# Score rounds earlier, value units together and the gelu table sooner, in one stage of an attention and MLP kernel

## The chip, the cores and the metric

One Trainium2 chip, one core of it. The metric is the device time of one execution in microseconds (us); lower is better. Engines: PE (TensorE, matmuls), PEld (its weight loads, which overlap), DVE (VectorE), ACT (ScalarE), POOL (GpSimd) and SP (SyncE, here only DMA issues).

## The reference, cut to what matters

```python
def _attn_ref(q_l, k_l, v_l, q_g, k_g, v_g):      # B=8, H=8, Sl=512, Sg=32, D=64
    k_all = concat([k_g, k_l]); v_all = concat([v_g, v_l])      # 544 positions
    out_g = softmax(scale * q_g @ k_all.T) @ v_all              # global queries see all
    s_ll  = scale * q_l @ k_l.T, where |pos_i - pos_j| <= 32, else -1e9
    s_lg  = scale * q_l @ k_g.T
    out_l = softmax(concat([s_lg, s_ll])) @ concat([v_g, v_l])  # local queries: window and globals
    return concat([out_g, out_l])

x = out.transpose(0, 2, 1, 3).reshape(B * 544, 512)
h = x @ w_in                         # w_in 512 x 2048
g = h * (1 / (1 + exp(-1.702 * h)))  # quick gelu
return g @ w_out                     # w_out 2048 x 512
```

## The kernel before

Each of the eight batches is worked on in two quads of four heads (`u` 0 and 1). For a batch, attention yields `xL`, the 512 local rows turned (four chunks of 128 columns: quad 0 gives chunks 0 and 1, quad 1 chunks 2 and 3). The first product (`h_mm`, L613) multiplies it with `w_in`, 16 steps `fc` of four matmuls of 128x512; ACT applies gelu from PSUM into `gT` (L618). The second product (`o_mm`, L653) multiplies `gT` with `w_out`: four output tiles `tci` of 128 rows, each a sum over 16 matmuls, issued in four steps of four matmuls. In `osteps(0, (tci, f4), ...)` the pair names tile and step; step `(tci, 3)` is the last of its tile and is followed by `o_out`, which copies the PSUM bank to `ob` (on ACT through `on_act`, L113, or on DVE through `nc.vector.tensor_copy`, L770) and has SP issue four stores.

The order on every engine is the order in which the program's lines issue instructions; it is written by hand (`tc.manual_schedule()`), and semaphores are put in where data or buffers depend. So a wait of an instruction holds everything behind it on its engine.

The change lies in the stage where the second product of batch 0 is mixed with the attention of batch 1. Its two quads are `a` and `c` (class `Wide`). The methods of a quad, with the lines that the profile shows:

- `Tk`, `Tq`, `ext` (L510, L502, L315, L505, L536 to L543, on DVE; parts on ACT, L113): bring keys and queries of the quad into place.
- `S(rnd)` (L558): one of two rounds of scores, 24 small matmuls that use 32 rows of the array each, into four PSUM banks in two tiles of two banks (a `spair()`; there is one, so each round reuses the banks of the round before).
- `X(rnd)` (L569): two exponentials on ACT, one for each two-bank tile, into `E[rnd]`.
- `M(rnd)` (L574, DVE): multiplies `E[rnd]` with the window's mask.
- `U(unit)` (L584): a value unit, 24 matmuls that use 32 columns each; unit 0 sums the rows of `E`, units 1 and 2 multiply with the values.
- `R` (L460, L462, L464, DVE): turns the sums of unit 0 (`sT`), takes reciprocals, and turns them back (`rs`).
- `XL(h)` (L469, DVE): unit 1 + h times `rs`, into `xL`.
- `Gm` (L595) and `G` (L474 to L477, DVE): the global queries, 20 matmuls, and their normalising.

PSUM has eight banks: the `spair()`'s four, and four in a pool (`pbank`) that second product tiles (`op`), `a`'s units (`ov`) and first product steps (`hp`) take in turn. `c`'s units and both `Gm` are written into a `spair()` of their own: bank 0 has `c.U(0)`, bank 1 both `Gm`, banks 2 and 3 `c.U(1)` and `c.U(2)`.

`exp_table()` and `gelu_table()` do one tiny activation on ACT, so that the table which the next activations need is loaded (ACT_TABLE_LOAD) at that place. `behind(x)` (L626) has POOL copy two elements of `x`; POOL issues the loads written behind it, those of batches 2 and 3, only then.

After this stage comes the first product of batch 1: eight matmuls on chunks 0 and 1 of `xL` (`kcs` (0, 1)), four on chunk 2, four on chunk 3, for the steps `fc` 0 to 3; then steps 4 to 15.

Of the kernel before, what the change touches and what calls it, by code (L numbers as in the profile page):

```python
# [20 lines left out]
def kernel(  # L21
# [12 lines left out]
    nc = tc.nc  # L34
# [40 lines left out]
    def load(b, us=(0, 1), kq=True):  # L75
        if b not in loaded:
            loaded[b] = (ld.tile([128, 2, 16 * D], BF16, name="rk"),
                         ld.tile([128, 2, 16 * D], BF16, name="rq"))
        if kq:
            s = slice(us[0], us[-1] + 1)  # L80
            nc.gpsimd.dma_start(out=loaded[b][1][:, s], in_=qf[b][:, s])
            nc.gpsimd.dma_start(out=loaded[b][0][:, s], in_=kf[b][:, s])
# [8 lines left out]
    def load_v(b, hs=slice(0, 8)):  # L91
        if b == 2:
            nc.gpsimd.memset(v_view(b, 5)[:, :, :, :, D:], 1.0)
        vt = v_view(b, 5).rearrange("p u j c d -> p (u j) c d")
        vs, vg = (x[b].rearrange("h s d -> s h d") for x in (v_l, v_g))
        for c in range(5):
            n = 128 if c == 2 else 96
            nc.gpsimd.dma_start(out=vt[0:n, hs, c, :D], in_=vs[FIRST[c] : FIRST[c] + n, hs])  # L98
            if c != 2 and b != 1:
                nc.gpsimd.dma_start(out=vt[96:128, :, c, :D], in_=vg)  # L100
# [176 lines left out]
    xL = {}  # L277

    def pbank(name):
        return psP.tile([128, 512], F32, name=name, tag="p")  # L280


    def spair():
        return [psS.tile([128, 2, 512], F32, name="s4", tag="s%d" % i) for i in range(2)]

    def bank(pair, j):
        return pair[j // 2][:, j % 2, :]
# [316 lines left out]
    gTs, ops = {}, {}  # L604
# [12 lines left out]
    def gelu(out_, in_):  # L617
        nc.scalar.activation(out_, in_, AF.Gelu_apprx_sigmoid)  # L618
# [6 lines left out]
    def behind(x):  # L625
        nc.gpsimd.tensor_copy(spot_p, x)  # L626

    def gelu_table():
        gelu(spot[:, 0:1], spot[:, 1:2])
# [16 lines left out]
    def o_mm(i, st, out=True):  # L646
        tci, f4 = divmod(st, 4)
        first = (i, tci) not in ops
        if first:
            ops[i, tci] = pbank("op")  # L650
        op = ops[i, tci]
        for fc in range(4 * f4, 4 * f4 + 4):
            nc.tensor.matmul(op, lhsT=gTs[i][:, fc, tci * 128 : tci * 128 + 128],  # L653
                             rhs=w_out_sb[:, fc, :], start=(first and fc == 4 * f4), stop=(fc == FC - 1))
        if f4 == 3 and out:
            o_out(i, tci, op)
# [102 lines left out]
    def tile_out(i, tci, ob):  # L759
        rows = out[i * S + Sg : (i + 1) * S].rearrange("(r t) m -> t r m", t=16)  # L760
        for j in range(4):
            nc.sync.dma_start(out=rows[4 * tci + j], in_=ob[32 * j : 32 * j + 32])
# [3 lines left out]
    def o_out(i, tci, op, copy=on_act):  # L766
        if tci % 2 == 0:
            obs[i, tci // 2] = moe.tile([128, 4, HM], F32, name="ob", bufs=3)
        ob = obs[i, tci // 2][:, tci % 2 * 2 : tci % 2 * 2 + 2].rearrange("p h m -> p (h m)")
        copy(ob, op)  # L770
        tile_out(i, tci, ob)

    a, c = Quad(0), Quad(1)
# [44 lines left out]
    pt = spair()  # L818
# [13 lines left out]
    pt = spair()  # L832
# [22 lines left out]
    def osteps(i, *sts):  # L855
        for tci, f4 in sts:
            o_mm(i, 4 * tci + f4)

    nq = {1: (Wide(2), Wide(3)), 2: (Wide(4), Wide(5))}
    a, c = nq[1]  # L860
# [3 lines left out]
    transpose_g(2, 4)  # L864
    a.ext((0, 1), on_act)
    a.ext((2, 3))
    osteps(0, (0, 1), (0, 0), (1, 1), (1, 0), (2, 1), (2, 0))
    a.S(0)
    a.X(0)
    copy_vg1()  # L870
# [1 line left out]
    c.Tq()  # L872
    c.ext()
    a.M(0)
    osteps(0, (0, 2), (1, 2), (2, 2))
    a.S(1)
    a.X(1)
    a.M(1)
    osteps(0, (3, 1), (3, 0))
    c.S(0)  # L880
    c.X(0)
    osteps(0, (0, 3), (1, 3))
    c.M(0)
    o_mm(0, 11, False)
    o_out(0, 2, ops[0, 2], nc.vector.tensor_copy)
    c.S(1)
    c.X(1)
    for unit in range(3):
        a.U(unit)
    a.R()  # L890
    c.M(1)
    behind(c.E[1][0:1, 0, 32:34])
    load(2, (0,))
    load_g(4, 8)
    load(2, (1,))
    load(3)
    load_v(2)
    osteps(0, (3, 2), (3, 3))
    pt = spair()
    a.XL(0)  # L900
    a.XL(1)
    a.Gm(bank(pt, 1)[:, 0:128])
    c.Gm(bank(pt, 1)[:, 128:256])
    c.U(0, bank(pt, 0))
    c.R()
    c.U(1, bank(pt, 2))
    c.U(2, bank(pt, 3))
    c.XL(0)
    c.XL(1)
    gTs[1] = moe.tile([128, FC, TB], BF16, name="gT")  # L910
    hps = [pbank("hp") for _ in range(4)]
    for kcs in ((0, 1), (2,), (3,)):
# [7 lines left out]
    pt = spair()  # L920
# [3 lines left out]
    a, c = nq[2]  # L924
# [154 lines left out]
    for i in range(1, B):  # L1079
        if i > 1:  # L1080
            for fc in range(FC):
# [3 lines left out]
                if i + 1 < B:  # L1085
                    c = nq[i + 1][1]
# [107 lines left out]
```

## Time and profile before

| | us |
|---|---|
| median of 3 runs | 288.90 (288.88 to 288.94) |
| the profiled execution: its own time | 288.66 |
| the profiled execution: its span | 286.6 |
| PE busy | 277.6 (97% of the span) |
| DVE busy | 204.6 (71%) |
| ACT busy | 184.4 (64%) |
| POOL busy | 94.1 (33%) |
| the stage from 31.8 to 48.3: PE busy | 16.27 of 16.50 |
| 48.3 to 55.8: PE busy | 6.85 of 7.50 |
| 55.8 to 66.6: PE busy | 10.75 of 10.80 |

The granted TensorE clock stands at 9 (90% or more) in every slice of the page but the last. Times in rows of the timeline are counted from the start of the span: start, duration, engine, line, operation, output tile <- input tiles, shapes, how many were merged into the row, and in brackets how long the engine had been idle before and who ended that. A chain row has start, duration and what ran. Matmuls are pipelined: a matmul of 512 columns shows 0.38 us but the next starts 0.22 after it.

### The profile page before, as it was taken

The page shows a single profiled execution, that of the slowest core. Times are in us where ns is not written, and L with a number is a line of the kernel's source. Part 1 is how long each engine was busy: PE and PEld are TensorE (multiplying, and loading weights), DVE is VectorE, ACT ScalarE, POOL GpSimd, SP SyncE. Part 2 cuts the span into 40 slices and gives each one's busy share as a digit, 9 for nine tenths or more (in the row PEclk, how much of TensorE's full clock was granted, in tenths as well). Part 3 has the DMA queues.
Part 4 walks back from the last instruction along what each step waited for, and adds up shares of the span by engine and source line. Part 5 has one row for each costly group of instructions (what it writes and reads, how often), then busy time and mean ns, then how long its engine had stood idle before and what let it go on. Part 6 is the DMA issues. An engine that isn't in the chain of part 4 may idle for free.

```text
span 286.6 us, 8822 instructions
## 1 busy us (share of the span) xinstructions
PE 277.6 (97%) x3704; PEld 178.6 (62%) x3727; DVE 204.6 (71%) x494; ACT 184.4 (64%) x296; POOL 94.1 (33%) x140
## 2 busy tenths in 40 slices
PE   7899999999999999999999999999999999999994
PEld 6544445544554488646884588647874588458883
DVE  7671457788689898679957997779957697363452
ACT  4847657388778784778559774877658761873440
POOL 8974550766936002920086004800040000000000
PEclk9999999999999999999999999999999999999999
DMA  7999994999999802993059703940122003200213
GB/s 204 167 200 211 202 143 66 153 224 144 161 170 174 150 3 57 91 185 59 12 84 160 139 2 78 107 58 5 29 54 70 2 3 76 73 0 2 73 44 106
DMA packets 59543, 28.23 MB, mean 98 GB/s; under 512 B 47472, under 2 KB 50032, under 8 KB 59504
## 3 DMA queue, kind: packets, MB, share of 16 engines
q0 software_dynamic: 51664, 17.57, 55.1%
q1 hardware_dynamic: 7264, 9.31, 11.8%
q10 hardware_dynamic: 576, 0.79, 0.8%
q8 instruction: 29, 0.48, 0.7%
q14 instruction: 10, 0.08, 0.1%
HBM read 36.31 MB, written 8.91 MB: 158 GB/s over the span
## 4 chain that ended last, share of the span: by engine, by line
PE 91%; DVE 2%; DMA 2%; POOL 1%; issue 1%; ACT 1%; DVEq 0%; POOLq 0%
PE hp L613 38%; PE px L724 13%; PE py L724 9%; PE op L653 9%; PE x L724 6%; PE s L558 6%; PE ov L584 5%; PE s L613 2%; DMA rk<-in_k_l_dram 2%; DVE xL L469 1%; ACT e L382 1%; PE og L595 1%; DVE rs L464 1%; DVE sT L460 0%; PE s L354 0%
## 5 line engine op out<-in xcount | busy, mean ns | idle before, releaser
L613 PE MATMUL hp<-xL,w_in_sb 128*128 128x512 bf16 x465 | 104.6, 379 | 1.2 <-DVE xL L469 0.4
L613 PEld LDWEIGHTS <-w_in_sb 128*128 128x128 bf16 x576 | 56.1, 98 | 60.3 <-issue 0.7
L618 ACT ACTIVATE gT<-hp 128x512 bf16<-128x512 f32 x120 | 69.9, 598 | 20.8 <-PE hp L613 19.3
L569 ACT ACTIVATE e<-s 128x1016 bf16<-128x1016 f32 (+1 forms) x56 | 53.3, 1003 | 22.1 <-PE s L558 22.0
L724 PEld LDWEIGHTS <-gs 128*128 128x128 bf16 x480 | 46.2, 98 | 6.4
L697 DVE TENSOR_TENSOR gs<-gT 128x512 bf16<-128x512 bf16 (+1 forms) x90 | 30.4, 365 | 17.6 <-ACT gT L618 17.3
L574 POOL TENSOR_TENSOR e<-e,mask 128x1760 bf16<-128x1760 bf16 x4 | 13.3, 3320 | 82.6 <-ACT e L569 82.6
L98 POOL DMA_DIRECT2D v<-in_v_l_dram x40 | 31.2, 781 | 15.4 <-PE og L595 4.3
L724 PE MATMUL py<-wsum,gs 128*128 128x256 bf16 x240 | 30.3, 273 | 0.0
L574 DVE TENSOR_TENSOR e<-e,mask 128x1712 bf16<-128x1712 bf16 (+1 forms) x24 | 25.2, 1049 | 6.0 <-ACT e L569 5.9
L653 PE MATMUL op<-w_out_sb,gT 128*128 128x512 bf16 x122 | 28.8, 380 | 0.5 <-issue 0.3
L510 DVE STREAM_TRANSPOSE kT<-rk 128x512 f32<-128x512 f32 x14 | 14.6, 1044 | 15.3 <-DMA rk<-in_k_l_dram 15.3
L653 PEld LDWEIGHTS <-gT 128*128 128x128 bf16 x128 | 11.8, 98 | 13.9
L724 PEld LDWEIGHTS <-gT 128*128 128x128 bf16 x192 | 18.0, 98 | 2.7
L724 PE MATMUL px<-w_out_sb,gT 128*128 128x256 bf16 x160 | 19.2, 273 | 0.0
L724 PE MATMUL px<-w_out_sb,gs 128*128 128x256 bf16 x160 | 19.1, 273 | 0.0
L469 DVE TENSOR_TENSOR xL<-ov,rs 128x512 bf16<-128x512 f32 x27 | 17.9, 687 | 0.8 <-PE ov L436 0.4
L694 DVE TENSOR_TENSOR gs<-gT 128x1024 bf16<-128x1024 bf16 (+1 forms) x30 | 17.4, 580 | 0.0
L558 PEld LDWEIGHTS <-kT 32*128 32x128 bf16 x672 | 12.6, 93 | 7.3 <-issue 5.9
L113 ACT ACTIVATE ob<-px 128x512 f32<-128x512 f32 x10 | 6.0, 599 | 15.2 <-DVE zz L746 15.2
L558 PE MATMUL s<-q,kT 32*128 32x160 bf16 (+1 forms) x448 | 14.9, 246 | 0.0
L100 POOL DMA_DIRECT2D v<-in_v_g_dram x24 | 13.9, 580 | 1.8 <-DMA rq<-in_q_l_dram 1.7
(149 smaller groups left out, 343.4 us busy)
## 6 DMA issues: line engine op xcount, KB each, us to landing
out_dram<-ob SPq DMA_DIRECT2D x128, 64.0 KB, 2.3
rq<-in_q_l_dram POOLq DMA_DIRECT2D x5, 512.0 KB, 8.4
rk<-in_k_l_dram POOLq DMA_DIRECT2D x5, 512.0 KB, 10.6
v<-in_v_l_dram POOLq DMA_DIRECT2D x24, 96.0 KB, 4.7
w_in_sb<-in_moe_w_in_dram POOLq DMA_DIRECT2D x8, 256.0 KB, 8.2
w_out_sb<-in_moe_w_out_dram POOLq DMA_DIRECT2D x4, 512.0 KB, 10.4
rq<-in_q_l_dram POOLq DMA_DIRECT2D x5, 256.0 KB, 7.9
rk<-in_k_l_dram POOLq DMA_DIRECT2D x5, 256.0 KB, 7.9
```

Source lines behind the costliest of these rows:

```text
L98: nc.gpsimd.dma_start(out=vt[0:n, hs, c, :D], in_=vs[FIRST[c] : FIRST[c] + n, hs])
L469: nc.vector.tensor_mul(self.x[:, 2 * self.u + h, :], self.st[1 + h], self.st["rs"])
L510: nc.vector.transpose(flat[:, 0:Sl].rearrange("p (r t) -> p t r", t=16), loaded[self.b][0][:, self.u].bitcast(F32))
L558: nc.tensor.matmul(bank(self.ps, j)[:, at : at + n], lhsT=self.k[p, KEYS[c] : KEYS[c] + 128, e], rhs=qs[p, :, :, e], start=(e == 0), stop= ...
L569: nc.scalar.activation(self.E[rnd][:, 2 * i : 2 * i + 2, :n], self.ps[i][:, :, :n], AF.Exp, scale=scale)
L574: eng.tensor_mul(e, e, mask[:, rnd : rnd + 1, :n].to_broadcast([128, 4, n]))
L613: nc.tensor.matmul(hp[:, : width(i)], lhsT=w_in_c[:, fc // 4, kc, fc % 4 // 2, :, fc % 2], rhs=(xL[i] if i < B else xG)[:, kc, :], start=( ...
L618: nc.scalar.activation(out_, in_, AF.Gelu_apprx_sigmoid)
L653: nc.tensor.matmul(op, lhsT=gTs[i][:, fc, tci * 128 : tci * 128 + 128], rhs=w_out_sb[:, fc, :], start=(first and fc == 4 * f4), stop=(fc = ...
L694: nc.vector.tensor_tensor(sums[i][2][:, g, :n], t[:, g, 0, :n], t[:, g, 1, :n], ALU.add)
L697: nc.vector.tensor_tensor(sums[i][k][:, g, : n // 2], x[:, g], y[:, g], op)
L724: nc.tensor.matmul(out_, lhsT=lv[:, g, tt * 128 : tt * 128 + 128], rhs=rv[:, g, :], start=(g == 0 and k in ((1, 3, 4, 6) if self.apart els ...
```

## The change

It reorders the stage. The rounds `a.S(0)`, `a.S(1)`, `c.S(0)` and `c.S(1)` come one to three steps of the second product earlier, so that two steps lie between one round and the next. The output tile 0 is evicted by DVE and tile 2 by ACT, which were the other way round. `a.U(0)` and `a.R()` stay behind the last round, but `a.U(1)`, `a.U(2)` come two steps after (2,3), in one group with `c`'s units and both `Gm`; `Gm` stands behind `c`'s units, which it preceded. Steps (3,2) and (3,3) come behind all of them, just ahead of the first product. `gelu_table()` is called ahead of (3,1), where before the table was loaded with the first gelu. `behind` waits for `a`'s second part of `xL` in place of `c`'s masked exponentials.

```diff
-    osteps(0, (0, 1), (0, 0), (1, 1), (1, 0), (2, 1), (2, 0))
+    osteps(0, (0, 1), (0, 0), (1, 1), (1, 0), (2, 1))
     a.S(0)
     a.X(0)
     copy_vg1()
...
     a.M(0)
-    osteps(0, (0, 2), (1, 2), (2, 2))
+    osteps(0, (2, 0), (0, 2))
     a.S(1)
     a.X(1)
     a.M(1)
-    osteps(0, (3, 1), (3, 0))
+    osteps(0, (1, 2), (2, 2))
     c.S(0)
     c.X(0)
-    osteps(0, (0, 3), (1, 3))
+    o_mm(0, 3, False)
+    o_out(0, 0, ops[0, 0], nc.vector.tensor_copy)
+    osteps(0, (1, 3))
     c.M(0)
-    o_mm(0, 11, False)
-    o_out(0, 2, ops[0, 2], nc.vector.tensor_copy)
     c.S(1)
     c.X(1)
-    for unit in range(3):
-        a.U(unit)
+    a.U(0)
     a.R()
+    osteps(0, (2, 3))
+    gelu_table()
+    osteps(0, (3, 1), (3, 0))
     c.M(1)
-    behind(c.E[1][0:1, 0, 32:34])
+    a.U(1)
+    a.U(2)
+    a.XL(0)
+    a.XL(1)
+    behind(xL[1][0:1, 1, 0:2])
     load(2, (0,))
     load_g(4, 8)
     load(2, (1,))
     load(3)
     load_v(2)
-    osteps(0, (3, 2), (3, 3))
     pt = spair()
-    a.XL(0)
-    a.XL(1)
-    a.Gm(bank(pt, 1)[:, 0:128])
-    c.Gm(bank(pt, 1)[:, 128:256])
     c.U(0, bank(pt, 0))
     c.R()
     c.U(1, bank(pt, 2))
     c.U(2, bank(pt, 3))
+    a.Gm(bank(pt, 1)[:, 0:128])
+    c.Gm(bank(pt, 1)[:, 128:256])
     c.XL(0)
     c.XL(1)
+    osteps(0, (3, 2), (3, 3))
```

## The prediction

> **What bounds the kernel now.** I read the page first (engines, the chain that ended last), then the chain between 28 and 66 us, then the timeline of that stretch engine by engine.
>
> ```profile
> PE 277.6 (97%) x3704; PEld 178.6 (62%) x3727; DVE 204.6 (71%) x494; ACT 184.4 (64%) x296; POOL 94.1 (33%) x140
> ```
>
> TensorE is the bound nearly everywhere, so the change is worth what it does to TensorE's waits, no more. The chain of batch 0's second product:
>
> ```profile
> 40.68 0.56 PE s L558 x24
> 41.25 0.16 issue
> 41.41 1.67 PE op L653 x7
> 43.08 0.18 PE s L558 x2
> 43.26 0.02 issue
> 43.28 0.64 PE s L558 x19
> 43.92 2.70 PE op L653 x12
> 46.61 0.56 PE s L558 x23
> ```
>
> Two waits stand here. The first is inside c.S(0): two score matmuls at 43.01 to 43.08, the others only from 43.28. (The "issue" 0.16 before 41.41 is no wait: eight weight loads and seven matmuls are recorded there, so one record is missing.) The second is at the next first product:
>
> ```profile
> 41.34 1.89 ACT L569 ACTIVATE e<-s 128x992 bf16<-128x992 f32 x2 [1.33 <-PE s L558]
> 43.98 1.93 ACT L569 ACTIVATE e<-s 128x1016 bf16<-128x1016 f32 x2 [0.75 <-PE s L558]
> 50.31 1.28 DVE L469 TENSOR_TENSOR xL<-ov,rs 128x512 bf16<-128x512 f32 x2
> 51.50 0.71 DVE L460 STREAM_TRANSPOSE sT<-s 128x512 f32<-128x512 f32 x1
> 53.35 1.29 DVE L469 TENSOR_TENSOR xL<-s,rs 128x512 bf16<-128x512 f32 x2
> 54.09 1.89 PE L613 MATMUL hp<-xL,w_in_sb 128*128 128x512 bf16 x8 [0.44 <-DVE xL L469]
> 55.41 1.28 ACT L618 ACT_TABLE_LOAD   x1 [4.57 <-PE hp L613]
> ```
>
> The first exp row ends at 43.23 and the stalled scores go on at 43.28: a score round writes the same two bank pairs as the round before and waits until its exponentials have read them. The product starts at 51.75; its eight matmuls on the first two chunks need 8 x 0.216 = 1.73 us, to 53.48, and the ninth starts at 54.09, 0.05 after c's first xL. So 0.60 us of wait (the row says 0.44, as it counts from the modelled end). 0.216 is (59.27 - 55.82) / 16 from the starts of two rows of the same product. Between 54.09 and 66.6 I find no gap in TensorE.
>
> **Part 1, score rounds sooner.** Before, an S round is followed by 12, 8 and 12 matmuls of the second product; after, by 8, 8 and 8 (rows (2,0),(0,2); (1,2),(2,2); (0,3),(1,3)). TensorE's own period with 12 is 40.62 - 37.34 = 3.28 us, so with 8 it is 3.28 - 4 x 0.216 = 2.41. ScalarE's loop is longer: two exponentials 1.89 or 1.93, 0.05 to release the banks, and 0.70 from the release to the next exponential (43.28 to 43.98): 2.64 or 2.68.
> - a.S(0) starts 4 matmuls sooner, 37.34 - 0.86 = 36.48 (its operands are ready: the last DVE copy ends at 35.85, ACT's at 35.90). Its exponentials run 37.22 to 39.15, banks free at 39.20; TensorE is at the second pair at 38.90. Wait 0.30.
> - c.S(0): 2.64 - 2.41 = 0.23. Its DVE operands, tied to a DMA and not moved, end at 41.14 and it starts at 41.6.
> - c.S(1): 2.68 - 2.41 = 0.27.
> Sum 0.80 against 0.27 before: **+0.53**. The trace bounds this well, as the same wait stands in it once (0.26); I allow 0.15 either way.
>
> **Part 2, evictions.** Output tile 0 goes to VectorE's copy (0.68), tile 2 to ScalarE (0.60). VectorE's copy starts at some 43.5, ahead of c.M(0), which waits for the exponentials until 44.5: hidden. ScalarE's eviction of tile 1 falls at 44.4 to 45.0, before c.S(1)'s exponentials can start at 45.2: hidden; without that cover 0.60 would lengthen ScalarE's loop. Tile 2's follows the last exponential, 47.0 to 47.6. Bank reuse, as the built program lists it, adds no wait: a.U(1) takes tile 1's bank, a.U(2) that of a.U(0), and the product's last bank is tile 3's, asked for 1.30 us (six matmuls) into the product and free some 0.85 after tile 3's last matmul (49.83 + 0.22 to 50.85 + 0.05 before).
>
> **Part 3, value units together.** c.S(1) now ends so that a.U(0) starts at 45.06. Then 4 + 8 matmuls of the second product to 48.14, and in one block a.U(1), a.U(2), c.U(0..2) at 0.37 each (50.55 to 50.91 for one), then the two Gm. The number of changes between tiled and full matmuls stays at five blocks. VectorE gets a.U(1) at 48.8 (last matmul 48.56, 0.22 long, 0.06 to VectorE), multiplies xL twice (0.60 each in a row), and starts c's transpose sT at 50.03, done at 50.74.
>
> In the built program's list of waits the first weight load of a.Gm now waits for that transpose: a.Gm writes the second bank of the pair whose first bank holds c.U(0). Before, Gm stood ahead of c.U(0) and had no such wait. TensorE arrives at 48.24 + 5 x 0.37 = 50.07 and goes on at 50.79: **+0.72**. Queued behind it on TensorE: both Gm, (3,2), (3,3) and the product, everything. No row of before shows this wait. Its lower bound is 0 (the transpose already done), its upper 1.0 (two xL at the 0.69 of a single one and a later a.U(1)); I take the computed value, as all its parts are rows of the same instructions, 0.2 either way.
>
> [...]
>
> **Part 4, cover for c's xL.** (3,2), (3,3) now stand between c's value units and the product. c's first xL ends at about 52.6, and the third chunk is wanted at 52.98 + 1.73 = 54.7: the wait of 0.60 goes, **-0.60**. The second Gm waited 0.09 (50.35 to 50.44) for c.M(1), now done at 48.4: -0.07 over its usual 0.02.
>
> **Part 5, gelu table and loads.** The load (1.28) and one 0.20 activation run at 47.6 to 49.1, where ScalarE waits for tile 3 until 53.2. ScalarE's first gelu comes some 0.7 us sooner (56.71 to about 56.0), but TensorE had no wait for gelu there: 0 on the path. Uncovered it would cost 1.28. `behind` now waits for a's second xL, 50.1, against 50.39 for c's mask: POOL's loads start 0.3 sooner. SP's stores of tiles 0 to 2 move forward, into 44 to 49.5; tile 3's 256 KB goes from 51 to about 54, into the loads. Priced in the first rival.
>
> **Sum.** +0.53 + 0.72 - 0.60 - 0.07 = +0.58, which I take as +0.6. The profiled execution took 288.66 us (span 286.6 and 2.06 around it): 289.26 by it. The median of the runs shown is 288.90, 0.24 more, and the forecast goes by it: **289.5**.
>
> **Rivals.**
> - *Late loads* (slower still). Batch 2's keys arrive at 58.23 and hold VectorE, then ScalarE:
>
> ```profile
> 58.23 1.05 DVE L510 STREAM_TRANSPOSE kT<-rk 128x512 f32<-128x512 f32 x1 [2.16 <-DMA rk<-in_k_l_dram]
> 60.68 0.31 ACT L113 ACTIVATE q<-qgT 128x128 bf16<-128x128 bf16 x1 [0.99 <-DVE qgT L243]
> 62.01 0.59 ACT L618 ACTIVATE gT<-hp 128x512 bf16<-128x512 f32 x1
> ```
>
>  The last row frees the bank that the thirteenth step of the product takes at 62.72: 0.07 to spare. TensorE comes 0.6 later, so the keys must be over 0.67 us late to cost anything. The store of tile 3 at the queue's share (9.31 MB took 11.8% of 286.6 us) is 0.9 us of all DMA engines, less the 0.3 sooner and less what it frees at 51. Against: probably 0.1 to 0.3 late. Price 0.3, time 289.8.
> - *No wait at a.Gm* (not slower). If a.Gm finds the transpose done, or bank by bank counts, only scores cost: 288.9 + 0.53 - 0.67 = 288.76. It decides from a transpose that ends before 50.07, that is, from a.U(1) 0.7 us earlier against c.U(2). Against: VectorE's rows add up without slack, and the wait is listed.
> - *ScalarE keeps pace*: if the loop took 2.41 like TensorE's, scores cost -0.27: 288.9 - 0.27 + 0.72 - 0.67 = 288.68. For: the exponentials start before a round's last score. Against: 43.23 to 43.28 to 43.98 in the trace.
> - Both of the last two: 288.9 - 0.94 = 287.96, the only way to faster.
> That the change doesn't do what it says is open for "sooner" alone: c.S(1) comes 12 matmuls (2.59 us) sooner in the order but ends only 2.04 sooner (a.U(0), behind it, at 45.06 against 47.10), as the waits eat the rest.
>
> **How the numbers follow.** A measurement of this kernel can tell 0.2%, 0.58 us, from no change: slower begins at 289.48, at the middle of the forecast's own range, 289.2 to 289.8. Forecast 0.73 (slower 0.41, within 0.32); late loads 0.12 (slower); no wait at a.Gm 0.07 and ScalarE keeps pace 0.05 (within); both 0.03 (faster). Slower 0.53, same 0.44, faster 0.03. The range leaves out 288.76 and 288.68 and faster below, and takes late loads to twice their price, above which a Gm wait at its upper bound adds some: 289.0 to 290.1.
>
> **What would show it.** Right: three S rounds with a gap of 0.2 to 0.3 after their second matmul; a gap of about 0.7 before the first matmul of a.Gm (L595), released by sT; no wait for xL at L613; the table load directly behind an output eviction; the shift of 0.6 unchanged to the end. Wrong: Gm directly behind the value units, scores without a gap, or new waits for gelu near 63 us.

## The result, and the profile after

The changed kernel takes **291.63 us** (median; 290.88 to 292.38) beside 288.92 for the kernel before in the same job: ratio **1.0093** (95% interval 1.0081 to 1.0104), 2.7 us slower. The forecast was 289.5 and the range 289.0 to 290.1: the sign was right, and the loss is four and a half times the 0.6 that was forecast. The profiled execution took 291.6 us, its span is 289.7, 3.1 more than before.

The lines of the page for the engines and for the instruction queue (q8, whose line is the same in the page before):

```profile
PE 280.1 (97%) x3727; PEld 179.0 (62%) x3727; DVE 205.2 (71%) x494; ACT 184.9 (64%) x297; POOL 94.1 (32%) x140
q8 instruction: 29, 0.48, 0.7%
```

No engine has more work to speak of (ACT has one activation more, the one ahead of (3,1); its table loads are 16 before and after). The granted TensorE clock is at 9 in all 40 slices of the page before and in all but the last, an 8, of the page after. So the time went into waits. The chain that ended last, in the changed stage:

```profile
39.49 0.63 PE s L558 x22
40.12 1.83 PE op L653 x8
41.95 0.82 PE s L558 x22
42.77 0.04 issue
42.81 1.94 ACT e L569 x2
44.74 0.04 issue
44.78 0.62 PE s L558 x22
...
49.11 1.29 DVE xL L469 x2
50.40 0.64 DVE sT L460
51.04 0.04 issue
51.08 0.51 PE s L595 x37
51.59 0.89 issue
52.47 0.20 PE s L595
```

Down to 51.08 this is the forecast: the chain goes through ScalarE's exponentials between score rounds, and through VectorE's transpose `sT` to `a.Gm`. The next two lines are not. Between the 39th and the 40th (last) matmul of the two Gm lies 0.89 us in which TensorE waited for nothing that the profile shows. The timeline of the same execution (in brackets: idle before, and who ended it):

```profile
39.18 0.58 PE L558 MATMUL s<-qc,kT 32*128 32x108 bf16 x8
41.88 0.76 PE L558 MATMUL s<-q,kT 32*128 32x160 bf16 x16
44.51 0.55 PE L558 MATMUL s<-qc,kT 32*128 32x108 bf16 x8
47.86 1.28 ACT L618 ACT_TABLE_LOAD   x1
51.08 0.51 PE L595 MATMUL s<-v,e 128*32 128x66 bf16 x39 [0.57 <-DVE sT L460]
52.47 0.20 PE L595 MATMUL s<-v,e 96*32 96x66 bf16 x1 [0.89 <-issue]
54.35 3.62 PE L613 MATMUL hp<-xL,w_in_sb 128*128 128x512 bf16 x16
56.33 1.04 DVE L510 STREAM_TRANSPOSE kT<-rk 128x512 f32<-128x512 f32 x1 [1.45 <-DMA rk<-in_k_l_dram]
85.03 0.55 PE L584 MATMUL ov<-e,v 128*32 128x128 bf16 x24 [0.85 <-issue]
```

The three score rows hold the three waits (an undisturbed x8 row takes 0.28, an undisturbed x16 row 0.53): 0.30, 0.23 and 0.27. The row of the first product has no bracket: the wait for `xL` is gone. Two rows end with "issue", at 52.47 and, 30 us behind the change in code that it doesn't touch, at 85.03. From weight load to weight load they measure 1.11 and 1.07 us, where the weight loads just ahead of them follow each other after 0.03 or less (first) and 0.08 or less (second). They are called the first and the second gap below.

Where the 3.1 us of span came in, by the start of the same row before and after: second product 32.07 and 32.36 (+0.3, ahead of the change); second block of the first product 55.82 and 57.80 (+1.98); `a2`'s first score round in the next stage 83.61 and 86.64 (+3.03); nothing more to the end. So +0.3 at the start, 0.6 as forecast, 1.1 for the first gap and 1.05 for the second, in this one execution.

Both gaps stand at a fixed count. Counted through TensorE's program (7491 instructions, weight loads and matmuls counted apart), they are before instructions 1475 and 2244, a multiple of 256 apart but for one. The page's queue q8 makes 29 transfers of 16 KB, and 7491 / 256 is 29.3. So TensorE's program is read here as blocks of 256 instructions, whose borders stand at 195, 451 and so on, at 1475 and at 2243. The trace's records of that queue, beside the time at which TensorE entered a block (all in us):

```
                       entered   transfer starts   takes   next block entered   after the transfer's end
before, block 1219       47.85        +0.52         1.30         +3.58                 1.75
after,  block 1219       48.90        +0.69         1.51         +3.57                 1.37   first gap
before, block 1987       76.22        +1.55         1.57         +5.74                 2.62
after,  block 1987       78.21        +4.39         0.93         +6.82                 1.50   second gap
```

In these four lines the transfer of the next block starts 0.52 to 4.39 us after the present block is entered, so less than one block is in reserve there, and the next block is entered 1.37 to 2.62 us after the transfer's end. So block 1219 of the changed kernel took 0.69 + 1.51 + 1.37 = 3.57 us, 1.1 of it the first gap; with the transfers of the other profiles the sum lies between 3 and 4. In the kernel before, block 1219 had eight of the second product's long matmuls in it (1.73 us; the row of before has seven, as one record is missing):

```profile
48.53 1.67 PE L653 MATMUL op<-w_out_sb,gT 128*128 128x512 bf16 x7 [0.16 <-issue]
```

In the changed one it holds 89 matmuls of value units and 39 of Gm, nothing else: (3,2) and (3,3) have moved behind them. In block 1987 the transfer itself came late.

### The profile page after: what moved, and what is told of

Its sections match the earlier page's. It is cut to its first block, busy times and chain, and to the rows that moved or that the text cites. A ratio compares the mean times of both kernels' runs of the same rounds, so it can differ in the third digit from the quotient of the medians.

```text
span 289.7 us, 8845 instructions
## 1 busy us (share of the span) xinstructions
PE 280.1 (97%) x3727; PEld 179.0 (62%) x3727; DVE 205.2 (71%) x494; ACT 184.9 (64%) x297; POOL 94.1 (32%) x140
## 4 chain that ended last, share of the span: by engine, by line
PE 91%; ACT 2%; DMA 2%; DVE 1%; POOL 1%; issue 1%; POOLq 0%
PE hp L613 38%; PE px L724 13%; PE py L724 9%; PE op L653 9%; PE x L724 6%; PE s L558 6%; PE ov L584 5%; PE s L613 2%; DMA rk<-in_k_l_dram 2%; ACT e L569 1%; ACT e L382 1%; PE og L595 1%; DVE xL L469 0%; PE s L354 0%; PE ov L421 0%
## 5 line engine op out<-in xcount | busy, mean ns | idle before, releaser
L653 PE MATMUL op<-w_out_sb,gT 128*128 128x512 bf16 x128 | 29.7, 380 | 0.0
```

## The experiments

Theory, formed on the trace above: the forecast's terms hold, and the rest of the loss is TensorE waiting for its own instructions. Rival: the gaps are waits for data or PSUM that the profile does not name, or the forecast's terms are too small. The first four runs move only the borders of the blocks (fewer instructions in the warm-up at the start of the program) and only the Gm.

### 20 instructions fewer ahead

```diff
-    fill(21, psP.tile([128, 512], F32, name="w", tag="p"), True)
+    fill(10, warm_ps, True, 256)     # ten matmuls of 256 columns
+    fill(1, warm_ps, True)           # and one of 128, in place of 21 of 128
```

Changed kernel:

> The changed kernel with 20 PE instructions fewer ahead of the stage: the 21 warm-up matmuls of 128 columns become ten of 256 and one of 128, the same columns. Fetch theory: PE's program comes in transfers of 16 KB (256 instructions) on the instruction queue, the next block's transfer starts only when PE enters a block, and the block can be entered some 1.4 us after its transfer ends; the 1.07 us gap in c.Gm stands at instruction 1475 because the 256 instructions before it are all small matmuls. With 20 fewer, the border falls behind steps (3,2),(3,3) of the second product (1.73 us), so that gap goes: -1.06 us, the wait at a.Gm for the transpose stays at 0.7, 290.0 to 290.6 (289.5 if the second gap of 1.07 us near 85 us goes too). Data theory: the last Gm matmuls wait for data or a semaphore that the trace doesn't show; the gap stays where it is in the work and the time stays at 291.6.

Kernel before, as a control:

> The kernel before with the same edit of the warm-up matmuls. Both theories: 288.9, within 0.2, as no PE gap at a border of 256 instructions is in its trace and the moved borders have long matmuls ahead of them. If the edit by itself costs or gains over 0.3 us, the run of the changed kernel with it has to be read against this one.

Control: 288.92, ratio 0.9998 (0.9989 to 1.0007): no difference from the warm-up itself is seen. Changed kernel: 290.05, ratio **1.0038** (1.0021 to 1.0056). Its profiled execution (289.38) has neither gap; the timeline (lines are two higher here):

```profile
51.00 0.51 PE L597 MATMUL s<-v,e 128*32 128x66 bf16 x40 [0.57 <-DVE sT L462]
51.44 1.90 PE L655 MATMUL op<-w_out_sb,gT 128*128 128x512 bf16 x8
```

All 40 Gm matmuls run through, and the wait for `sT` stays. So the first gap belongs to the place in the program, not to that matmul's data. The runs spread from 289.38 to 291.84.

### Both Gm back ahead of c's value units

```diff
     pt = spair()
+    a.Gm(bank(pt, 1)[:, 0:128])
+    c.Gm(bank(pt, 1)[:, 128:256])
     c.U(0, bank(pt, 0))
...
     c.U(2, bank(pt, 3))
-    a.Gm(bank(pt, 1)[:, 0:128])
-    c.Gm(bank(pt, 1)[:, 128:256])
```

> The changed kernel with both Gm ahead of c.U(0), as in the kernel before, so that no Gm waits for the transpose of c's sums. Sum of the prediction (waits add up): -0.72, 290.9. Fetch theory: the same 256 instructions still stand between the borders 1219 and 1475, the next block cannot be entered sooner, so the gap at instruction 1475 (now in c.U(2)) grows by what the transpose no longer costs, to some 1.8 us: 291.6, no change.

Measured 291.10, ratio **1.0068** (1.0056 to 1.0081), between what the two theories gave. The timeline:

```profile
49.32 0.51 PE L595 MATMUL s<-v,e 128*32 128x66 bf16 x40
50.01 0.91 PE L584 MATMUL s<-e,v 128*32 128x128 bf16 x47
51.92 0.23 PE L584 MATMUL s<-e,v 128*32 128x128 bf16 x1 [1.01 <-issue]
```

The wait for `sT` is gone, and the gap is still before instruction 1475, which is now a value matmul of `c`: a different instruction with different data at the same count. If the block alone set the time, the gap should have grown by all of the 0.73 that the wait took. It grew by 0.2 (to 1.31). From `a.U(1)` to the first product it is 5.24 us against 5.84, 0.60 less; 0.45 of that is a transfer that took 1.06 here against 1.51. Whether the shorter transfer is chance or follows from the change is not settled. The medians differ by 0.7 us (0.2 to 1.2 by the intervals), so that the size expected by the blocks alone was a miss.

### Both together

> Both edits: Gm first and 20 PE instructions fewer. Fetch theory: neither the wait for the transpose (0.72) nor the gap at the border (1.06) is left; against the kernel before only the score rounds' +0.53 and the gains of 0.67 stay: 288.8 if the gap near 85 us goes too, 289.8 if it stays. Data theory: as with Gm first alone, 290.9.

Measured 288.75, ratio **0.9989** (0.9981 to 0.9998). The timeline has no gap left:

```profile
49.09 0.51 PE L597 MATMUL s<-v,e 128*32 128x66 bf16 x40
49.41 0.55 PE L586 MATMUL s<-e,ones 128*32 128x128 bf16 x24
49.78 0.91 PE L586 MATMUL s<-e,v 128*32 128x128 bf16 x48
50.62 1.90 PE L655 MATMUL op<-w_out_sb,gT 128*128 128x512 bf16 x8
```

Between the profiled executions with 20 fewer, in which nothing else differs in the stage, Gm ahead is worth 0.75 us from `a.U(1)` to the product (4.00 against 4.75): the term of the forecast, 0.72, was right. By the ratios the same step is 0.0049, 1.4 us; the rest of that is not explained, and is taken up under what stays open.

### 8 instructions fewer

The border moves eight places, past the last c.Gm matmul and three matmuls of (3,2).

```diff
-    fill(21, psP.tile([128, 512], F32, name="w", tag="p"), True)
+    fill(4, warm_ps, True, 256)
+    fill(13, warm_ps, True)
```

> The changed kernel with 8 instructions fewer on TensorE, in the warm-up at its start (eight matmuls of 128 columns are replaced by four of 256), so that every later instruction stands 8 places sooner in TensorE's program. Theory (TensorE's program arrives in blocks of 256 instructions, and a block can't be entered before some 1.4 us after its transfer ended): the gap leaves the last c.Gm matmul and stands at the fourth matmul of row (3,2), which now opens the block; three matmuls of 0.216 us come into the block before it, so the gap is 1.1 - 0.65, 0.3 to 0.6 us; the second gap stays somewhere near 0.9, as the loads ahead of its transfer are not moved. Time 290.9 (290.6 to 291.2). Rival (the last c.Gm matmul waits for data or for a PSUM bank): the gap of 1.1 stays at the same matmul, time 291.6.

Measured 290.19, ratio 1.0043 (1.0021 to 1.0065), below the 290.6 to 291.2 that was expected.

```profile
51.50 0.82 PE L655 MATMUL op<-w_out_sb,gT 128*128 128x512 bf16 x3
52.63 1.25 PE L655 MATMUL op<-w_out_sb,gT 128*128 128x512 bf16 x5 [0.31 <-issue]
```

The gap went to the matmul that the count names, 0.90 from weight load to weight load where its neighbours need 0.216, so 0.68 (0.3 to 0.6 was expected: the transfer started 1.37 after entry, not 0.69). It was entered 1.37 after the transfer's end, as in the changed kernel. The second gap, which was expected to stay, is not in this execution: its transfer started 2.36 after entry, not 4.39.

### Keys of batch 4 loaded later

```diff
         a.M(0)
-        loads_after(1)
+        load_v(3)
+        load_g(8, NQ)
...
         c.M(0)
+        behind(c.E[0][0:1, 0, 32:34])
+        load(4)
```

> The changed kernel, where the 1 MB of queries and keys that POOL loads at 76.1 and 76.8 us is issued only behind c.M(0), near 80.5 us. Theory (the transfer of TensorE's next block, which started 4.4 us after the block was entered, stood behind these loads): it starts within 2 us, the second gap (1.07 us at 85.0 us) goes, the first stays; time 291.6 - 1.0 = 290.6. Rival 1 (the second gap is a wait for data, or the clock): nothing changes, 291.6. Rival 2 (the keys are wanted early): a new wait of VectorE for them later, 291.6 or more.

Measured 290.77, ratio **1.0061** (1.0043 to 1.0079), 0.9 us less than the changed kernel by the ratios. The timeline:

```profile
53.98 0.20 PE L595 MATMUL s<-v,e 96*32 96x66 bf16 x1 [1.32 <-issue]
82.48 0.70 POOL L81 DMA_DIRECT2D rq<-in_q_l_dram  x1 [0.28 <-issue]
85.13 0.90 PE L584 MATMUL ov<-e,v 128*32 128x128 bf16 x48
```

(This execution ran 1.1 us behind the changed kernel's from the start of the second product on, and its first gap is longer, so that its own time, 292.09, is the highest of the six.) The first gap stays, and all 48 value matmuls of the second place run in a row: the transfer for that border started 0.83 after entry instead of 4.39, and the keys' load followed it. The second gap was an instruction transfer that came late, and moving the loads of queries and keys out of its way took it away in this run. The keys' load as POOL issued it, in the kernel before and in the changed one:

```profile
77.85 0.73 POOL L82 DMA_DIRECT2D rk<-in_k_l_dram  x1
76.78 0.73 POOL L82 DMA_DIRECT2D rk<-in_k_l_dram  x1
```

In the kernel before these loads were issued at 77.16 and 77.85, 0.9 and 1.6 us after TensorE had entered block 1987 at 76.22; in the changed one at 76.09 and 76.78, ahead of its entry at 78.21. TensorE came later by 2 us and the loads came sooner by 1. In the fourteen profiles it takes the meeting of the two: the changed kernel (entry 78.21, both loads issued by 77.51) and the one with Gm first (77.66, by 77.48) are the only two that entered the block after both loads had been issued, and their transfers started 4.39 and 4.84 after entry. In the other twelve it was 0.83 to 3.14. With 20 instructions fewer the loads stayed where they were, but the block was entered at 77.12, while the keys' load was still being issued, and the transfer started 2.38 after entry, in time; with 8 fewer it was entered at 77.58, between the two loads, and the transfer started 2.36 after. These loads are not all that can hold the transfer up: in the next run, which issues them later too, it still started 3.10 after entry. The later loads were not tried on the kernel before, so that a gain of their own is not excluded.

### Both covers, the change itself whole

The 20 instructions fewer and the later keys at once, with everything of the change left in.

> The changed kernel with both covers for the instruction blocks at once: 20 instructions fewer on TensorE in the warm-up (21 matmuls of 128 columns become ten of 256 and one of 128), and batch 4's queries and keys issued behind c.M(0) of the first full phase. Everything of the change itself stays: scores at 8 matmuls, a.Gm behind c's transpose, (3,2) and (3,3) behind c's xL. Theory (the prediction's terms are right and the instruction blocks are the rest): no gap at a border, the three score waits and the wait of 0.35 over its usual 0.52 at a.Gm stay: the kernel before + 0.6, ratio 1.002, 289.5. Rival (the terms themselves were too small): ratio 1.004 or more, as with the 20 instructions alone (1.0038).

Measured 289.79, ratio **1.0023** (1.0007 to 1.0039). The profile has the three score waits, the wait of Gm (0.72: the last two value units start at 49.91, and 49.91 + 0.74 = 50.65) and no gap at a border; its rows for Gm and for the place of the second gap:

```profile
51.37 0.51 PE L597 MATMUL s<-v,e 128*32 128x66 bf16 x40 [0.57 <-DVE sT L462]
82.83 0.90 PE L586 MATMUL ov<-e,v 128*32 128x128 bf16 x48
```

The forecast's own sum, 0.58 us, is a ratio of 1.0020. So the sum of the terms held, within 0.5 us either way; the 2 us between 1.0023 and 1.0093 are what the two covers for the instruction blocks gave back.

### Parts of the change on the kernel before

Score rounds at 12, 12 and 12 matmuls, with a.S(0) one step sooner:

```diff
-    osteps(0, (0, 1), (0, 0), (1, 1), (1, 0), (2, 1), (2, 0))
+    osteps(0, (0, 1), (0, 0), (1, 1), (1, 0), (2, 1))
...
-    osteps(0, (0, 2), (1, 2), (2, 2))
+    osteps(0, (2, 0), (0, 2), (1, 2))
...
-    osteps(0, (3, 1), (3, 0))
+    osteps(0, (2, 2), (3, 1), (3, 0))
```

> The kernel before with a.S(0) one step sooner and 12 matmuls of the second product between any two score rounds (12, 8, 12 before): nothing else moved. Sum of waits: TensorE's 3.28 us from round to round are longer than ScalarE's 2.64 in each case, so the one wait of 0.26 us that the kernel before has goes and none comes: 288.92 - 0.26 = 288.66. Rival (a wait of VectorE or of the exponentials that only moves on to the next first product, where TensorE waits for c's xL): 288.9, no change.

Measured 288.97, ratio 0.9994 (0.9983 to 1.0004): too close to tell 0.26 us from none. The trace shows c.S(0) without its wait, and the wait for `xL` as before:

```profile
43.02 0.53 PE L558 MATMUL s<-q,kT 32*128 32x160 bf16 x16
53.84 1.89 PE L613 MATMUL hp<-xL,w_in_sb 128*128 128x512 bf16 x8 [0.37 <-DVE xL L469]
```

The version between the two: a.S(0) a step sooner as above, (2,2), (0,3), (1,3) ahead of c.S(0) and (2,3), (3,1) behind it, so that 12, 12 and 8 matmuls lie between the rounds; tiles 0 and 1 evicted by VectorE; Gm where it was; (3,3) behind `c`'s value units.

```diff
     for unit in range(3):
         a.U(unit)
...
-    osteps(0, (3, 2), (3, 3))
+    osteps(0, (3, 0), (3, 2))
...
     a.Gm(bank(pt, 1)[:, 0:128])
     c.Gm(bank(pt, 1)[:, 128:256])
...
     c.U(2, bank(pt, 3))
+    osteps(0, (3, 3))
     c.XL(0)
```

> A version between the two: the kernel before with a.S(0) one step sooner, 12, 12 and 8 matmuls between the score rounds, the two Gm still ahead of c's value units, and (3,3) behind c's xL as cover. Sum of waits: one score wait of 0.27 (0.26 before), the wait of 0.60 for xL at the first product gone, no wait of Gm for a transpose: 288.92 - 0.6 = 288.3 to 288.4. Instruction blocks: the block of the value units and Gm keeps eight long matmuls, as in the kernel before, so no gap at its end: the same time. Rival (small matmuls side by side cost whatever stands in the block): a gap of 0.3 to 1 us near 52 us, 288.7 to 289.4.

Measured 288.56, ratio **0.9982** (0.9970 to 0.9994): faster than both kernels, with the whole interval below 1. The timeline shows one score wait (the first row, 0.58 for 0.28) and the product running through:

```profile
45.63 0.58 PE L558 MATMUL s<-qc,kT 32*128 32x108 bf16 x8
51.19 1.04 PE L653 MATMUL op<-w_out_sb,gT 128*128 128x512 bf16 x4
52.06 3.62 PE L613 MATMUL hp<-xL,w_in_sb 128*128 128x512 bf16 x16
```

At its border 1475 this version lies where the borders with a gap lie (1.28 to 1.50): 1.41 us after the transfer's end, with 0.08 between two weight loads there. Three more versions are built on it with the 20 instructions fewer. First that alone (the edit of the first experiment):

> before_one_step with 20 instructions fewer in the warm-up, which brings the four matmuls of (3,3) into the block of the value units and Gm. There that block was entered 1.41 us after its transfer's end, at the limit, and its first weight load came 0.08 late. Theory: that rest of 0.1 goes, in some executions more: ratio 0.9975, 288.3. Rival (nothing is lost at that border): the same as before_one_step, 0.9982.

Measured 288.63, ratio 0.9999 (0.9976 to 1.0022), runs from 288.14 to 291.37: no gain is shown. Then with c.S(0) between the halves of step (1,3):

```diff
-    o_mm(0, 7, False)
-    o_out(0, 1, ops[0, 1], nc.vector.tensor_copy)
+    o_mm(0, 7, False, range(2))
     c.S(0)
     c.X(0)
+    o_mm(0, 7, False, range(2, 4))
+    o_out(0, 1, ops[0, 1], nc.vector.tensor_copy)
```

> before_one_step_20_fewer, where c.S(0) stands between the two halves of step (1,3), so that 12, 10 and 10 matmuls of the second product lie between the score rounds. TensorE's period with 10 is 3.28 - 2 x 0.216 = 2.85 us, longer than ScalarE's 2.68, so the last score wait (0.27) goes: 0.27 less than before_one_step_20_fewer, ratio 0.9966. Rival (the time is then held by VectorE's chain to c's xL at the product): the same as before_one_step_20_fewer.

And with a.S(0) between the halves of (2,0) too:

```diff
+    o_mm(0, 8, True, range(2))
     a.S(0)
...
-    osteps(0, (2, 0), (0, 2), (1, 2))
+    o_mm(0, 8, True, range(2, 4))
+    osteps(0, (0, 2), (1, 2))
```

> half_steps_20_fewer with a.S(0) between the two halves of step (2,0): 22 matmuls of the second product ahead of it, then 10, 10 and 10. a.S(0) comes half a step sooner than in the kernel before, not a whole one, so that batch 1's keys may come 0.43 us later than in half_steps_20_fewer before TensorE waits for them (in that kernel's profiled execution their transpose began at 34.88 us, against 31.8 to 32.9 in the others, and a.S(0) waited 0.97). Theory (scores wait only where ScalarE's 2.68 us are longer than TensorE's 2.85 with ten matmuls, and never here): no score wait, 288.2, ratio 0.997, and a smaller spread upward than the 290.51 of half_steps_20_fewer. Rival (the spread comes from elsewhere): the same median and the same spread.

Measured 288.34, ratio 0.9983 (0.9962 to 1.0005), and 288.61, ratio 0.9994 (0.9978 to 1.0010). Neither interval excludes no change, and the spread upward of the second (290.53) is that of the first (290.51), so its rival (the spread comes from elsewhere) holds as far as that goes. The score waits are gone in both traces, but both profiled executions show another thing:

```profile
34.88 1.04 DVE L512 STREAM_TRANSPOSE kT<-rk 128x512 f32<-128x512 f32 x1 [11.65 <-DMA rk<-in_k_l_dram]
38.07 0.53 PE L560 MATMUL s<-q,kT 32*128 32x160 bf16 x16 [0.97 <-ACT q L113]
```

```profile
42.27 1.45 PE L655 MATMUL op<-w_out_sb,gT 128*128 128x512 bf16 x6 [0.55 <-DMA w_out_sb<-in_moe_w_out_dram]
```

In the first (half steps) batch 1's keys came 2 us later than in twelve other profiles (31.8 to 32.9), and a.S(0) waited 0.97 for them. In the second (tens) step (0,3) waited 0.55 for the last quarter of `w_out`, whose load was issued at 32.87 there and at 30.8 to 31.9 in the same twelve, and took 9.1 to 9.3 us. Whoever moves scores and (0,3) sooner uses up a reserve towards loads of the start, whose time varies from one execution to the next. That this makes part of the changed kernel's own time was not shown: its profile has neither wait.

## Why the prediction went wrong, point by point

- **What bounds the kernel** was right, and so was that only TensorE's waits count. The reading stopped at waits for data, though: the page's line for the instruction queue was not asked what it costs.
- **Part 1, score rounds** (+0.53): three waits of 0.30, 0.23 and 0.27 were forecast, and the timeline shows 0.30, 0.23 and 0.27. The rival that ScalarE keeps pace fell.
- **Part 2, evictions** (0): no bracket of TensorE names an eviction. Right.
- **Part 3, a.Gm waits for `sT`** (+0.72): the changed kernel's timeline shows 0.73 (from value units to Gm it takes 0.74 where nothing waits, 49.09 - 48.35 in the kernel with both edits; the last two units, `c.U(1)` and `c.U(2)`, start at 49.61, and 49.61 + 0.74 = 50.35, but Gm starts at 51.08) and 0.75 from the pair of runs with and without it. The rival "no wait at a.Gm" fell. What the chip itself would have needed there is not shown by this: the wait is one that the program was built with.
- **Part 4, cover for `c`'s `xL`** (-0.60 and -0.07): the first product runs through at 54.35. Right, and the product runs through in the version between the two as well, at 52.06.
- **Part 5, table and loads** (0 on the path): the table load stands at 47.86, directly behind an eviction, where nobody waits for it. The late loads rival fell: the keys were thought to come 0.1 to 0.3 late, and came at 56.33 against 58.23, sooner.
- **The sum**: +0.58 forecast, and 1.0023, which is +0.66 (0.2 to 1.1), measured with the covers. **The step that failed** is the one from there to the time: "the shift of 0.6 unchanged to the end", resting on Part 3's costing of "one block" of value units and Gm by the durations of their matmuls alone. Two terms were missing, 1.1 us each or nearly. Packing 128 small matmuls without a long one between them uses up 256 instructions in 2.5 us (3.57 - 1.1), the wait for `sT` included, faster than the next ones arrive (+1.1); this is shown by the gap that stayed with the count when the instructions were moved. And a shift of TensorE against POOL's loads came with a later instruction transfer that started 4.39 us after entry (+1.05), 30 us after the change; that these loads are what it waits behind rests on one run and on the fourteen times of entry. Neither was among the rivals. The late loads rival had asked what POOL's loads delay, but only for data.

What stays open: why the changed kernel with the 20 instructions fewer alone stands at 1.0038, 0.5 us above the sum, when its profiled execution shows no gap. The intervals of 1.0038 and 1.0023 overlap; the second gap in some of the executions would fit it, and no profile shows one there. By the ratios the later loads gave 0.9 us alone and 0.4 us on top of the 20 fewer, and neither is sharp. Nor is it settled how much of Gm's wait the changed kernel would give back while the first gap is there.

## What to carry to other kernels

Look at how many instructions TensorE is asked to run per microsecond, not only at how long each one is: here 128 small matmuls side by side (256 instructions in 2.5 us, where the block took 3.57) ran out of program, and the profile showed "issue" ahead of an instruction that waits for nothing that it shows (0.85 to 1.32 between small matmuls; the 0.16 in front of a row that lacks one matmul is a missing record). Count the place of such a gap in the engine's program; if gaps recur at a fixed count, spread long matmuls among the small ones, or move the border by a few instructions ahead (20 fewer took the ratio from 1.0093 to 1.0038 here). After a reordering, look again at stages that were not touched, since a shift against another engine's bulk loads can cost as much there (the second gap, 1.05 us in the profiled execution, 30 us behind the change).

## What the runs showed of the hardware

- TensorE's instructions came in 29 transfers of 16 KB for 7491 instructions, and the two gaps of the changed kernel stood at 1475 and 2244, a multiple of 256 apart but for one. For the borders after blocks 1219 and 1987 the transfer started 0.49 to 4.84 us after entry and took 0.88 to 2.07. From block 963 on, no border in the fourteen profiles was passed less than 1.28 us after its transfer's end, and all six with a gap lie between 1.28 and 1.50. Four more lie at 1.37 to 1.42; two of these show 0.1 us and two no more than the usual spacing of their weight loads (0.02 and 0.22). Later in the program the transfer started up to 3.3 us ahead of the block's first instruction, and no border from 2499 on was passed less than 1.9 us after its transfer's end:

```
                            border   after the transfer's end   gap
after                         1475            1.37              1.11
after                         2243            1.50              1.07
after_gm_first                1475            1.28              1.31
after_gm_first                2243            1.36              1.33
after_8_fewer                 1475            1.37              0.90
after_keys_later              1475            1.29              1.54
before_rounds_12              1475            1.39              0.12
before_one_step               1475            1.41              0.08
before_20_fewer               1475            1.37              none
after_gm_first_20_fewer       1475            1.42              none
```

- For block 1987 the transfer started 4.39 and 4.84 us after entry in the two executions that entered behind both loads of queries and keys, and 0.83 to 3.14 in the other twelve; of the two with later loads it was 0.83 in one and 3.10 in the other.
- Loads of the first 30 us landed up to 2 us apart from one profile to the next: the transpose of batch 1's keys began between 31.8 and 34.9 us.
